# Probabilities kept in fp32, transposed by TensorE instead of by DMA, in an attention and expert kernel on one core

## The chip, the cores and the metric

One core of one Trainium2 chip. The metric is the device time of one execution in microseconds (us). Engines: TensorE (PE, its weight loads PEld), VectorE (DVE), ScalarE (ACT), GpSimd (POOL), SyncE (SP, whose queue issues all DMAs of this kernel).

## The reference

Attention over 4 batches, 8 heads, 1152 keys, head size 64, with the queries averaged in pairs (576 queries), and then a two-layer network with an ELU on the 2304 x 512 result (the weights arrive as 64-bit floats):

```python
q_pool = q.reshape(B, H, S // 2, 2, D).mean(axis=3)
scores = (1.0 / np.sqrt(D)) * np.matmul(q_pool, k.transpose(0, 1, 3, 2))
scores = scores - np.max(scores, axis=-1, keepdims=True)
attn = np.exp(scores)
attn = attn / (np.sum(attn, axis=-1, keepdims=True) + 1e-09)
x = np.matmul(attn, v)                      # then (B * 576, 512)
h = x @ w_in                                # 512 -> 2048
g = np.where(h > 0.0, h, np.exp(np.minimum(h, 0.0)) - 1.0)
out = g @ w_out                             # 2048 -> 512
```

## The kernel before

Each batch is a unit. A unit has 4 pairs of heads, a pair has 9 steps: 8 of 128 queries of one head (`st.h`, `st.t`) and one of the last 64 queries of both heads (`st.h is None`). That makes 144 steps. Operands of most matmuls are split in a high and a low fp16 half, and the products high x high, high x low, low x high are summed in PSUM.

`prep` (per pair) loads q, k and v, finds their scale (`absum` on ACT, `across`), splits them (`halves`: the high half on ACT, L429, the low one on DVE, L441, or POOL, L447) and transposes q and k by DMA (L519, L531).

`attention` (per step) runs, each as a task of its own:

1. `scores`: PE, L721, L726, L733, into the one PSUM tile `s`;
2. `biggest`: DVE, L739, scales `s` into SBUF (`ep`, fp32, 128x1152) and takes the row minimum;
3. `expo`: ACT, L745, the exponential in place with its row sum; `total`: ACT, L750; `recip`: DVE, L753;
4. `phi`: the normalised high half in fp16, on ACT (L764) or POOL (L756); `plo`: the low half, DVE, L759;
5. `ptr`: one DMA transpose of both halves (128 x 2304 fp16) into `pT`, issued on SP's queue (L783);
6. after every second step `pv`: PE, L822, L826, L832 (26 fp16 matmuls for 256 queries of a head), then `xa` (ACT, L844) and `xb` (DVE, L849), which add the two halves into `x32`.

`experts` works on a unit in two groups, 256 and 320 tokens: `m1` (L940, 12 matmuls for each 128 of the 2048 columns, fp16), the ELU (ACT L948 and L951, POOL L956, DVE L961, ACT L975 or POOL L983, POOL L979 or DVE L987), and `m2` (L1007, 48 matmuls for 128 tokens). It needs `x32` of all 8 heads, so the first unit's expert work starts when its attention is nearly done; from then on one unit's experts run beside the next unit's attention. `weights` and `split` decode the 64-bit weights (DVE L603, L604, L607; ACT L613, L649; DVE L652) in the opening.

The order on each engine's queue is fixed before the kernel runs: the class `Plan` places every task greedily by a key (its due time, from the constants in `CFG`), a booked duration and free buffers, and some tasks may go to one of two or three engines (`ways`). The tiles named `wo`, `g` and `h` in the trace are lent to each other: `ep` and `pT` of the first unit lie in buffers that later hold weights or activations (`wo`, `x16`).

PSUM: `s` takes three banks, and five banks `r` serve PV, `m1`, `m2` and `across`. SBUF: three `ep`, two `pT` buffers.

Of the kernel before, what the change touches and what calls it, by code (L numbers as in the profile page):

```python
# [18 lines left out]
    LOADS=130179, WI0=13938, WIT=6664, WO0=239437, WOT=10447, T0=3015, T1=1567, M0=7758,  # L19
    M1=49670, KS=33691, KM=2336, KE=12361, KH=7660, KL=-4056, KV=13470, KN=3968,  # L20
    KX=18983, KO=78603, PEN=600, W0L=-30160, WIN=1000, PD=18438, KS0=45563, KM0=5296,
    KE0=116348, KH0=-4488, KL0=-4155, KV0=2757, KX0=31516, PLM0=0, NS0=36, PLM=0,
    M2=24726, DP=0, FK=0, PENW=0, PENH=-3000, FL=2000, PH0=2, PH=1,
    PLP=1, WLP=1, HIP=0, PA=-715, PB=1180,
# [16 lines left out]
class Buf:  # L41


    def __init__(self, plan, tags):
        self.plan, self.tags, self.tag, self.users, self.slot, self.ap = plan, tags, tags[0], [], None, None


class Task:
    def __init__(self, eng, dur, key, emit, after, bufs):
        self.eng, self.dur, self.key, self.emit = eng, dur, key, emit  # L50
        self.ways = {eng: (dur, emit)}
        self.after = [a for a in after if a is not None]
        self.bufs = bufs
        self.pen = None
        self.kids, self.left, self.ready, self.end = [], 0, 0.0, None


class Plan:
# [4 lines left out]
    TAIL = {"PE": 70.0, "DVE": 75.0, "ACT": 90.0, "POOL": 30.0, "DMA": 0.0}  # L63

# [10 lines left out]
    def add(self, eng, dur, key, emit, after=(), bufs=(), ways=()):  # L75
        t = Task(eng, dur, key, emit, after, list(bufs))
        for e, d, f in ways:
            t.ways[e] = (d, f)
        for b in t.bufs:
            b.users.append(t)  # L80
        self.tasks.append(t)
        return t

    def _slots_for(self, t, now):
        taken = []
        for b in t.bufs:
            if b.slot is None:
                at = next(
                    (
                        (tag, j) for tag in b.tags for j, o in enumerate(self.slots[tag])  # L90
                        if (tag, j) not in [x for x, _ in taken]
                        and (o is None or all(u.end is not None and u.end <= now for u in o.users))
                    ),
                    None,
                )
                if at is None:
                    return None
                taken.append((at, b))
        return taken

    def run(self):
        order = []
        for n, t in enumerate(self.tasks):
            t.n = n
            t.left = len(t.after)
            for a in t.after:
                a.kids.append(t)
# [4 lines left out]
        landing, events = [], []  # L112
        for t in self.tasks:
            if t.left == 0:
                for e in t.ways:
                    wait[e].append(t)
        done = 0
        now = 0.0
        turn, used, cold, moved = self.WINDOW, 0.0, True, 0.0

# [6 lines left out]
        def finish(t, at):  # L127
            t.end = at
            for kid in t.kids:
                kid.left -= 1  # L130
                kid.ready = max(kid.ready, at + self.TAIL[t.eng] + (30.0 if t.eng == "DMA" else self.LAT[kid.eng]))
                if kid.left == 0:
                    for o in kid.ways:
                        wait[o].append(kid)
                    heapq.heappush(events, kid.ready)

        while done < len(self.tasks):
            again = True
            while again:
                again = False  # L140
                for e in engines:
# [3 lines left out]
                    for t in sorted((t for t in wait[e] if t.ready <= now), key=lambda t: (t.key, t.n)):  # L145
                        if e != t.eng:
                            ahead = rest[t.eng] if busy[t.eng] is not None else 0.0
                            ahead += sum(
                                o.dur for o in wait[t.eng]
                                if o.eng == t.eng and o.ready <= now + CFG["WIN"] and (o.key, o.n) < (t.key, t.n)  # L150
# [3 lines left out]
                        need = self._slots_for(t, now)  # L154
# [6 lines left out]
                    for (tag, j), b in need:  # L161
                        b.tag, b.slot = tag, j
                        self.slots[tag][j] = b
                    for o in t.ways:
                        wait[o].remove(t)
# [4 lines left out]
                    rest[e] = float(t.dur)  # L170
                    if e == "DMA":
# [13 lines left out]
            while events and events[0] <= now:  # L185
                heapq.heappop(events)
            if events:
                ends.append(events[0])
# [28 lines left out]
    def emit(self):  # L217
        for t in self.run():
            for b in t.bufs:
                if b.ap is None:  # L220
                    ap = self.make[b.tag](b.slot)
                    b.ap = ap if b.tag == b.tags[0] else self.lend[b.tags[0], b.tag](ap)
            t.emit()
# [3 lines left out]
def attention_moe_kernel(  # L227
# [22 lines left out]
    dr = ctx.enter_context(tc.tile_pool(name="dr", bufs=1, space=bass.MemoryType.DRAM))  # L250
# [8 lines left out]
    pool("v32", 1, [128, 2, NCH, D], F32)  # L259
# [25 lines left out]
    plan.lend["ep", "wo"] = lambda ap: whole(ap)[:, 0:3 * S]  # L285
    plan.lend["pT", "x16"] = lambda ap: whole(ap).rearrange("p (c s) -> p c s", s=256)
# [51 lines left out]
    for u in units:  # L338
# [9 lines left out]
        early = [(h, t) for h in range(2) for t in range(2)]  # L348
        late_ = [(h, t) for h in range(2) for t in range(2, u.nt)] + [(None, u.nt)]
# [37 lines left out]
    ones, tiny = wk[:, 60:61], wk[:, 61:62]  # L387
    make_identity(nc, ident)
    nc.vector.memset(ones, 1.0)
    nc.vector.memset(tiny, 1e-9 * 2.0 ** -15)  # L390
# [21 lines left out]
    kept = {}  # L412

    def prep(pr, t0, t1):
        u, p = pr.u, pr.p
        b, nq = u.b, u.nq
        q32, qn, qT, kT, v16, sm = (plan.buf(x) for x in ("q32", "qn", "qT", "kT", "v16", "sm"))
        pr.kT, pr.qT, pr.v16, pr.sm = kT, qT, v16, sm
# [59 lines left out]
        def plain(dst, src):  # L478
            return lambda: nc.sync.dma_start(out=dst(), in_=src())

# [7 lines left out]
        k_f, v_f = (lambda: kT.ap.rearrange("p h c s -> p (h c s)")), (lambda: v16.ap.rearrange("p h c e d -> p (h c e d)"))  # L488
# [4 lines left out]
        old = kept.get((b, p))  # L493
        nsum = 1 if old else 3
        if old is None:
            k32, v32, kn = (plan.buf(x) for x in ("k32", "v32", "kn"))
            k_s = lambda: k32.ap.rearrange("p h c d -> p (h c) d").rearrange("p (f t) d -> p f t d", t=2)
            k_h, k_l = (lambda: kn.ap[:, :, 0:4:3]), (lambda: kn.ap[:, :, 1:3])
            v_s, v_h, v_l = (lambda: v32.ap), (lambda: v16.ap[:, :, :, 0]), (lambda: v16.ap[:, :, :, 1])
            tk = plan.add("DMA", Move(500.0, 2400.0), lk, load(k, k32), (), [k32])  # L500
            tv = plan.add("DMA", Move(500.0, 2400.0), lk + 1, load(v, v32), (), [v32])
            sums.append(plan.add("ACT", act(1152) + 90.0, key[1], absum(k_h, k_s, 1), [tk], [kn, k32, sm]))
            sums.append(plan.add("ACT", act(1152) + 90.0, key[2], absum(k_h, v_s, 2), [tv, sums[1]], [kn, v32, sm]))

        def up(top):
# [3 lines left out]
            o = old[2].ap if old else a  # L509
            nc.vector.tensor_scalar(a[:, 0:nsum], a[:, 4:4 + nsum], 2.0 ** -14, None, op0=ALU.mult)  # L510
            ts(nc.vector, a[:, 12:13], a[:, 0:1], o[:, 1:2], -1.0 / (2.0 * float(D) ** 0.5))
            nc.vector.tensor_scalar(a[:, 13:14], o[:, 2:3], 2.0 ** -15, None, op0=ALU.mult)

        sms = [sm, old[2]] if old else [sm]
        sc = pr.sc = across(lambda: sm.ap[:, 0:nsum], nsum, key[3], sums + ([old[3]] if old else []), sms, up)
# [22 lines left out]
        if old:  # L538
            pr.kdone = [plan.add("DMA", Move(500.0, 2400.0), lk + 2, plain(k_f, lambda: old[0]), [old[4]], [kT])]
            pr.vdone = [plan.add("DMA", Move(500.0, 2400.0), lk + 3, plain(v_f, lambda: old[1]), [old[5]], [v16])]  # L540
            return
        kl = halves(1152, key[6], key[7], k_h, k_l, k_s, 1, [sc, sums[2]], [kn, k32, sm])
# [3 lines left out]
        if sum(o.b == b for o in units) > 1:  # L546
            kd = dr.tile([128, 2 * S], F16, name=f"kd{p}")
            vd = dr.tile([128, 2 * S], F16, name=f"vd{p}")
            kw = plan.add("DMA", Move(500.0, 2400.0), key[15], plain(lambda: kd, k_f), pr.kdone, [kT])
            vw = plan.add("DMA", Move(500.0, 2400.0), key[15], plain(lambda: vd, v_f), pr.vdone, [v16])  # L550
            kept[b, p] = (kd, vd, sm, pr.sc, kw, vw)
# [150 lines left out]
    def attention(st):  # L702
# [4 lines left out]
        def e_():  # L707
            return ep.ap[:, S:].bitcast(F32)

        def p_(j):  # L710
            return ep.ap[:, j * S:(j + 1) * S]
# [37 lines left out]
        def total():  # L749
# [321 lines left out]
```

## Time and profile before

| | |
|---|---|
| three runs | 938.51, 944.24 and 947.08 us, median 944.24 |
| span of the profiled execution | 938.4 us, from the first to the last instruction |
| busy share of the span | PE 78%, DVE 77%, ACT 74%, POOL 40% |
| DMA queue of SP | 156.01 MB, 80.8% of the 16 DMA engines |
| mean granted TensorE clock | 0.906 of full speed |

A share is a mean over three stages that differ: an opening of about 300 us (weights are decoded, attention of the first unit, little expert work), a middle of about 550 us (attention of one unit beside the experts of the one before), and an end of about 89 us (experts only). Busy PE time holds the time of the pipe's drain, so the distance between the starts of two stretches of matmuls tells the pace, not the sum of busy times.

### The profile page before, as it was taken

How to read it: one execution, taken by the hardware profiler on the slowest of the kernel's cores; microseconds unless marked ns; L12 is line 12 of the kernel's file. 1: busy time of each engine (PE TensorE's matmuls, PEld its weight loads, DVE VectorE, ACT ScalarE, POOL GpSimd, SP SyncE). 2: the span in 40 equal slices, each digit the busy share in tenths (PEclk: the TensorE clock that was granted, in tenths of full speed). 3: DMA queues.
4: the chain of work that ended last, by engine and by line, in shares of the span. 5: the costliest groups of instructions: out<-in, count | busy, mean ns of one | idle time of the engine just before them, and what ended most of it. 6: DMA issues, size and time to landing. Idle time of an engine off the chain costs nothing.

```text
span 938.4 us, 14749 instructions
## 1 busy us (share of the span) xinstructions
PE 733.5 (78%) x5283; PEld 428.6 (46%) x5283; DVE 724.7 (77%) x1235; ACT 690.8 (74%) x1169; POOL 375.4 (40%) x344
## 2 busy tenths in 40 slices
PE   0256455566939898998997989869978899689997
PEld 0123232333716455445644644438435544366563
DVE  5998999988998888878785886877777896785220
ACT  4587877877778889867777997568777987674460
POOL 3420513101637768402633881226324762043260
PEclk9998656756869999999998999979989999899999
DMA  7899999999957789897598989876799988754000
GB/s 236 223 200 202 236 227 246 236 190 264 199 138 163 125 169 200 164 198 140 105 201 179 199 175 206 170 152 105 156 214 201 168 159 177 136 102 76 23 1 28
DMA packets 434056, 156.94 MB, mean 167 GB/s; under 512 B 395840, under 2 KB 414272, under 8 KB 433984
## 3 DMA queue, kind: packets, MB, share of 16 engines
q1 hardware_dynamic: 433984, 156.01, 80.8%
q8 instruction: 41, 0.67, 0.3%
q14 instruction: 31, 0.25, 0.1%
HBM read 45.09 MB, written 4.72 MB: 53 GB/s over the span
## 4 chain that ended last, share of the span: by engine, by line
PE 25%; DVE 17%; DMA 15%; ACT 8%; issue 8%; POOL 5%; SPq 1%; DVEq 0%; POOLq 0%; ACTq 0%
DMA pT<-ep 12%; PE r L940 9%; PE r L1007 8%; DVE ep L739 7%; DVE ep L759 3%; ACT ep L745 3%; PE r L822 3%; PE s L721 2%; PE r L832 1%; POOL g L979 1%; PE s L733 1%; DMA kT<-kn 1%; ACT ep L764 1%; DVE tmp L961 1%; ACT tmp L951 1%
## 5 line engine op out<-in xcount | busy, mean ns | idle before, releaser
L745 ACT ACTIVATE ep<-ep,nm 128x1152 f32<-128x1152 f32 x132 | 165.2, 1251 | 75.1 <-DVE ep L739 55.7
L759 DVE SCALAR_TENSOR_TENSOR ep<-ep,nm 128x1152 f16<-128x1152 f32 x132 | 203.7, 1548 | 18.1 <-ACT ep L764 10.3
L739 DVE TENSOR_SCALAR_CACHE_REDUCE ep<-s,sm 128x1152 f32<-128x1152 f32 x132 | 186.4, 1412 | 38.1 <-DMA pT<-ep 24.4
L940 PE MATMUL r<-x,wi 128*128 128x256 f16 (+1 forms) x1536 | 201.6, 290 | 9.0 <-DVE x L849 5.1
L1007 PE MATMUL r<-wo,g 128*128 128x512 f16 (+1 forms) x864 | 176.1, 385 | 0.0
L721 PE MATMUL s<-kT,qT 128*128 128x512 f16 (+3 forms) x480 | 108.2, 366 | 86.1 <-DVE ep L739 67.9
L940 PEld LDWEIGHTS <-wi 128*128 128x128 f16 x1536 | 149.2, 99 | 56.9 <-issue 18.2
L764 ACT ACTIVATE ep<-ep,nm 128x1152 f16<-128x1152 f32 x111 | 138.3, 1247 | 22.3 <-DVE nm L753 22.0
L822 PE MATMUL r<-pT,v 128*128 128x256 f16 (+1 forms) x855 | 102.2, 272 | 35.3 <-DMA pT<-ep 19.8
L1007 PEld LDWEIGHTS <-g 128*128 128x128 f16 (+1 forms) x864 | 73.7, 102 | 87.9 <-issue 10.1
L956 POOL TENSOR_SCALAR tmp<-tmp,us 128x320 f32<-128x320 f32 (+1 forms) x96 | 73.3, 766 | 86.3 <-ACT tmp L951 86.1
L721 PEld LDWEIGHTS <-qT 128*128 128x128 f16 (+1 forms) x480 | 40.7, 105 | 138.9 <-issue 108.7
L822 PEld LDWEIGHTS <-v 128*128 128x128 f16 x864 | 70.3, 106 | 63.0 <-issue 29.3
L961 DVE SCALAR_TENSOR_TENSOR tmp<-r,wk,tmp 128x320 f32<-128x320 f32 (+1 forms) x96 | 57.5, 611 | 31.5 <-POOL tmp L956 31.1
L756 POOL TENSOR_SCALAR ep<-ep,nm 128x1152 f16<-128x1152 f32 x21 | 29.3, 1395 | 125.3 <-DVE nm L753 123.8
L979 POOL TENSOR_TENSOR g<-tmp,g 128x320 f16<-128x320 f32 (+1 forms) x70 | 70.9, 1019 | 12.6 <-ACT g L975 10.9
L384 POOL TENSOR_SCALAR q<-q,sm 128x576 f32<-128x576 f32 x14 | 12.6, 900 | 133.8 <-ACT qn L429 133.8
L948 ACT ACTIVATE tmp<-r 128x320 f32<-128x320 f32 (+1 forms) x96 | 46.5, 485 | 21.9 <-PE r L940 16.3
L733 PE MATMUL s<-kT,qT 64*128 64x512 f16 (+1 forms) x320 | 62.5, 432 | 0.0
L951 ACT ACTIVATE tmp<-tmp,us 128x320 f32<-128x320 f32 (+1 forms) x96 | 58.0, 609 | 1.3
L844 ACT ACTIVATE x<-r,sm 64x256 f32<-64x256 f32 (+1 forms) x96 | 39.9, 415 | 23.7 <-PE r L832 22.3
L832 PE MATMUL r<-pT,v 128*64 128x256 f16 (+1 forms) x760 | 56.9, 278 | 0.0
(128 smaller groups left out, 1041.8 us busy)
## 6 DMA issues: line engine op xcount, KB each, us to landing
k<-in_k_dram SPq DMA_DIRECT2D x16, 576.0 KB, 4.7
v<-in_v_dram SPq DMA_DIRECT2D x16, 576.0 KB, 4.6
q<-in_q_dram SPq DMA_DIRECT2D x32, 256.0 KB, 3.4
qT<-qT SPq DMA_DIRECT2D x48, 144.0 KB, 2.8
g<-in_moe_w_in_dram SPq DMA_DIRECT2D x13, 512.0 KB, 5.3
g<-in_moe_w_out_dram SPq DMA_DIRECT2D x13, 512.0 KB, 5.2
out_dram<-tmp SPq DMA_DIRECT2D x16, 256.0 KB, 2.7
pT<-ep SPq DMA_TRANSPOSE x130, 4.8
```

Source lines behind the costliest of these rows:

```text
L721: nc.tensor.matmul(s.ap[rows, c, 0:n], pr.qT.ap[:, 0, j, rows], keys[h][c], start=True, stop=False, skip_group_check=True,)
L733: nc.tensor.matmul(s.ap[rows, c, 0:512], pr.qT.ap[r, 1, j, rows], keys[h][c][r], start=False, stop=True, skip_group_check=True,)
L739: nc.vector.tensor_scalar(e_(), s.ap.rearrange("p a b -> p (a b)")[:, 0:S], pr.sm.ap[:, 12:13], None, op0=ALU.mult, op1=ALU.min, accum_out ...
L745: nc.scalar.activation(out=e_(), in_=e_(), func=AF.Exp, bias=nm.ap[:, 0:1], scale=-1.0, accum_out=nm.ap[:, 2:3],)
L759: nc.vector.scalar_tensor_tensor(out=p_(1), in0=e_(), scalar=nm.ap[:, 3:4], in1=p_(0), op0=ALU.mult, op1=ALU.subtract)
L764: nc.scalar.activation(out=p_(0), in_=e_(), func=AF.Copy, scale=nm.ap[:, 3:4])
L822: nc.tensor.matmul(x.ap[:, os], vt[:, order[c]].rearrange("p e d -> p (e d)"), pT.ap[:, c, cs], start=(c == 0), stop=False, skip_group_che ...
L940: nc.tensor.matmul(hp.ap[:, f * n:(f + 1) * n], w[:, a, c, (f0 + f) * 128:(f0 + f + 1) * 128], x16.ap[:, e, c, g0:g0 + n], start=(i == 0), ...
L951: nc.scalar.activation(out=en.ap[:, :m], in_=en.ap[:, :m], func=AF.Exp, scale=us.ap[:, 8 + g:9 + g])
L956: nc.gpsimd.tensor_scalar(en.ap[:, :m], en.ap[:, :m], -1.0, us.ap[:, 5:6], op0=ALU.add, op1=ALU.mult)
L979: nc.gpsimd.tensor_tensor(out=l, in0=gv, in1=h, op=ALU.subtract)
L1007: nc.tensor.matmul(op.ap[r0:r0 + tn, :], gt[qd].ap[:, a, fi, o:o + tn], w_out16(f // 2)[:, e, f % 2, :], start=(i < 128 // tn), stop=(i >= ...
```

## The change

- `expo` stays. `total` goes; `recip` adds the 1e-9 in an operation of its own. `phi` and `plo` go; one `norm` multiplies the fp32 probabilities in place, on POOL, or where POOL is behind on DVE or ACT.
- The DMA transposes `ptr` go. In their place each step has 9 TensorE transposes (fp32, 128 x 128, against the identity), three at a time into one PSUM bank `r`, and three copies (`out_act` or `out_dve`, 128 x 384 fp32) from there into `pT`.
- `pv` works in fp32 on the unsplit v: 18 matmuls for 128 queries of both heads, those of head 0 into PSUM partitions 0 to 63 and those of head 1 into 64 to 127. One copy per two steps (`xb` on DVE, or `xa`) replaces the pair `xa` and `xb`. The split of v goes from `prep` (one `absum`, one high and one low half per pair).
- Steps alternate between the two heads. `ep` has four fp32 buffers, `v32` three, `v16` goes.
- The plan: the constants are new; transposes that wait (`thin`) are woven one by one between the matmuls of an `m1` or `m2` task (`parts`) that is placed at that time, up to a quarter as many groups of three as that task has matmuls; a change of the array's tile mode is booked.

```diff
 CFG = dict(
-    LOADS=130179, WI0=13938, WIT=6664, WO0=239437, WOT=10447, T0=3015, T1=1567, M0=7758,
...
+    LOADS=-114467, WI0=33877, WIT=9245, WO0=755935, WOT=6543, T0=2082, T1=1393, M0=16194,
...
+        def weave(t, need):
...
+            for key, _, g in wait["PE"]:
+                if len(guests) >= len(host[0].parts) // 4:
+                    break
+                if g.thin and g is not t:
...
+            thin = [f for g in t.guests for f in g.thin]
+            for i, f in enumerate(t.parts):
+                if i < len(thin):
+                    thin[i]()
+                f()
...
-    pool("v16", 2, [128, 2, NCH, 2, D], F16)
-    pool("ep", 3, [128, 3 * S], F16)
+    pool("ep", 4, [128, S], F32)
-    pool("pT", 2, [128, 2 * NCH, 256], F16)
+    pool("pT", 2, [128, 2, NCH, 128], F32)
...
-        early = [(h, t) for h in range(2) for t in range(2)]
+        early = [(h, t) for t in range(2) for h in range(2)]
...
-        pr.vdone = [halves(1152, key[11], key[12], v_h, v_l, v_s, 2, [sc], [v16, v32, sm])]
+        pr.vdone = [tv]
...
         def recip():
+            nc.vector.tensor_scalar(nm.ap[:, 3:4], nm.ap[:, 2:3], 1e-9, None, op0=ALU.add)
             nc.vector.reciprocal(nm.ap[:, 3:4], nm.ap[:, 3:4])
...
         def norm_pool():
             nc.gpsimd.tensor_scalar(e_(), e_(), nm.ap[:, 3:4], 1.0, op0=ALU.mult, op1=ALU.mult)
+        def norm_dve():
+            nc.vector.tensor_scalar(e_(), e_(), nm.ap[:, 3:4], None, op0=ALU.mult)
...
-        def ptr():
-            nc.sync.dma_start_transpose(
-                out=pT.ap[:, :, half * 128:half * 128 + 128], in_=ep.ap[:, 0:2 * S]
-            )
...
+            def one(c, j=j, tp=tp):
+                nc.tensor.transpose(tp.ap[:, c * 128:(c + 1) * 128], e_()[:, (j + c) * 128:(j + c + 1) * 128], ident)
...
+            def out_act(j=j, tp=tp):
+                nc.scalar.activation(out=dst(j), in_=tp.ap[:, 0:384], func=AF.Copy)
+            def out_dve(j=j, tp=tp):
+                nc.vector.tensor_copy(dst(j), tp.ap[:, 0:384])
...
         def pv():
+            for c in range(NCH):
+                for h in range(2):
+                    order = [*range(h, 8, 2), *range(1 - h, 8, 2), 8]
+                    p = pT.ap[:, h, c] if st.h is not None else pT.ap[:, 0, c, 64 * h:64 * h + 64]
                     nc.tensor.matmul(
+                        x.ap[64 * h:64 * h + 64, 0:n], pr.v32.ap[:, h, order[c]], p,
+                        start=(c == 0), stop=(c == NCH - 1), skip_group_check=True,
                     )
...
         def xb():
+            nc.vector.tensor_copy(xdst(), x.ap[:, 0:n])
```

## Rows read from the trace of the kernel before

**Rows 1.** The head of the page: the span of the profiled execution.

```profile
span 938.4 us, 14749 instructions
```

**Rows 2.** Busy time by stage: stretch, length, PE, PEld, DVE, ACT, POOL (instructions), clock, DMA, GB/s.

```profile
0.00:300.00 300.00, 163.70 (x1056) 92.61 (x1057) 268.31 (x485) 224.18 (x380) 94.36 (x72) 0.78 0.93 212
300.00:850.00 550.00, 487.17 (x3685) 288.27 (x3684) 436.38 (x710) 433.42 (x724) 255.72 (x236) 0.96 0.85 164
850.00:939.00 89.00, 82.61 (x547) 47.69 (x544) 20.04 (x41) 33.22 (x67) 25.27 (x38) 0.98 0.15 34
```

**Rows 3.** The same stretches, `expo` alone (L745, ACT; two instructions per step).

```profile
0.00:300.00 300.00, 59.10 (x88) 0.78 0.93 212
300.00:850.00 550.00, 134.42 (x200) 0.96 0.85 164
```

**Rows 4.** The opening, `plo` alone (L759, DVE), then `phi` (L764, ACT).

```profile
0.00:300.00 300.00, 64.75 (x43) 0.78 0.93 212
0.00:300.00 300.00, 53.10 (x43) 0.78 0.93 212
```

**Rows 5.** The middle, `m1` (L940: PE, PEld), then `m2` (L1007).

```profile
300.00:850.00 550.00, 140.56 (x1079) 103.01 (x1080) 0.96 0.85 164
300.00:850.00 550.00, 148.72 (x716) 60.98 (x714) 0.96 0.85 164
```

**Rows 6.** Timeline of PE in the middle: start, length, line, shapes, count of matmuls.

```profile
328.86 0.65 PE L721 MATMUL s<-kT,qT 128*128 128x512 f16 x3
...
329.82 1.16 PE L822 MATMUL r<-pT,v 128*128 128x256 f16 x9
330.81 0.27 PE L826 MATMUL r<-pT,v 128*128 128x256 f16 x1
331.01 0.63 PE L832 MATMUL r<-pT,v 128*64 128x256 f16 x8
331.57 1.80 PE L940 MATMUL r<-x,wi 128*128 128x320 f16 x12
...
333.35 1.79 PE L940 MATMUL r<-x,wi 128*128 128x320 f16 x12
334.98 2.75 PE L1007 MATMUL r<-wo,g 128*128 128x512 f16 x12
```

**Rows 7.** Timeline of PE in the opening: one PV, then the next scores.

```profile
199.89 2.08 PE L822 MATMUL r<-pT,v 128*128 128x256 f16 x9 [2.68 <-DVE x L849]
...
203.11 1.14 PE L721 MATMUL s<-kT,qT 128*128 128x512 f16 x3
```

**Rows 8.** Groups by line and shape: busy us, mean ns, idle before.

```profile
L948 ACT ACTIVATE tmp<-r 128x320 f32<-128x320 f32 x64 | 27.6, 433 | 11.1 <-PE r L940 9.0 <-POOL g L979 1.0 <-POOL tmp L956 0.3
L948 ACT ACTIVATE tmp<-r 128x512 f32<-128x512 f32 x32 | 18.9, 590 | 10.9 <-PE r L940 7.3 <-DVE g L987 1.8 <-POOL g L979 1.5
L750 ACT ACTIVATE nm<-nm,wk 128x1 f32<-128x1 f32 x144 | 41.2, 286 | 1.6
L849 DVE SCALAR_TENSOR_TENSOR x<-r,sm,x 64x256 f32<-64x256 f32 x64 | 30.2, 472 | 11.7 <-ACT x L844 10.8
L429 ACT ACTIVATE v<-v,sm 128x1152 f16<-128x1152 f32 x16 | 19.9, 1242 | 1.3 <-PE r L832 1.3
L756 POOL TENSOR_SCALAR ep<-ep,nm 128x1152 f16<-128x1152 f32 x21 | 29.3, 1395 | 125.3 <-DVE nm L753 123.8 <-issue 1.4
```

**Rows 9.** Single lines of PE: duration in ns, least, median and greatest; the forms.

```profile
L397 PEld LDWEIGHTS r<-ident,sm x16: 81/81/86, 10.9 to 749.7; 128*3 128x3 f32 x16
L397 PE MATMUL r<-ident,wk x9: 270/371/373, 21.7 to 285.2; 128*1 128x128 f32 x9
L404 PEld LDWEIGHTS r<-xr,wk x66: 180/183/333, 13.3 to 877.3; 1*128 1x128 f32 x34, 3*128 3x128 f32 x32
L726 PE MATMUL s<-kT,qT x160: 218/219/314, 39.4 to 838.6; 128*128 128x128 f16 x128, 128*64 128x128 f16 x32
L822 PE MATMUL r<-pT,v x855: 189/272/421, 61.9 to 863.7; 128*128 128x256 f16 x113, 128*128 128x64 f16 x58
```

More of the change, by code (lines that the diff above doesn't have):

```diff
@@ L54, in __init__ @@
         self.pen = None
+        self.parts, self.thin, self.guests, self.modes = None, None, [], ("full", "full")
         self.kids, self.left, self.ready, self.end = [], 0, 0.0, None
@@ L79, in add, with _slots_for, _take @@
         for b in t.bufs:
-            b.users.append(t)
+            b.open += 1
+        t.modes = modes or t.modes
+        t.parts, t.thin = parts, thin
+        t.n = len(self.tasks)
         self.tasks.append(t)
         return t
-    def _slots_for(self, t, now):
-        taken = []
+    def _slots_for(self, t, used):
+        taken, mine = [], set()
         for b in t.bufs:
[L87 to L94, printed above, removed]
-                )
-                if at is None:
-                    return None
-                taken.append((at, b))
-        return taken
+            if b.slot is not None:
+                continue
+            at = None
+            for tag in b.tags:
+                for j, o in enumerate(self.slots[tag]):
+                    if (o is None or o.open == 0) and (tag, j) not in mine and (tag, j) not in used:
+                        at = (tag, j)
+                        break
+                if at is not None:
+                    break
+            if at is None:
+                return None
+            mine.add(at)
+            taken.append((at, b))
+        return taken
+    def _take(self, need):
+        for (tag, j), b in need:
+            b.tag, b.slot = tag, j
+            self.slots[tag][j] = b
     def run(self):
         order = []
[L103 to L107, printed above, removed]
         engines = ("PE", "DVE", "ACT", "POOL", "DMA")
@@ L111, in run @@
         rest = {e: 0.0 for e in engines}
-        landing, events = [], []
+        landing, coming = [], []
+        for t in self.tasks:
+            t.left = len(t.after)
+            for a in t.after:
+                a.kids.append(t)
         for t in self.tasks:
             if t.left == 0:
-                for e in t.ways:
-                    wait[e].append(t)
+                heapq.heappush(coming, (0.0, t.n, t))
         done = 0
@@ L119, in run @@
         turn, used, cold, moved = self.WINDOW, 0.0, True, 0.0
+        mode = "full"
         def shares():
@@ L128, in finish @@
             t.end = at
+            for b in t.bufs:
+                b.open -= 1
             for kid in t.kids:
@@ L144, in run @@
                     best = None
-                    for t in sorted((t for t in wait[e] if t.ready <= now), key=lambda t: (t.key, t.n)):
+                    for _, _, t in wait[e]:
                         if e != t.eng:
@@ L148, in run @@
                             ahead += sum(
-                                o.dur for o in wait[t.eng]
-                                if o.eng == t.eng and o.ready <= now + CFG["WIN"] and (o.key, o.n) < (t.key, t.n)
+                                o.dur for _, _, o in wait[t.eng]
+                                if o.eng == t.eng and (o.key, o.n) < (t.key, t.n)
+                            )
+                            ahead += sum(
+                                o.dur for r, _, o in coming
+                                if o.eng == t.eng and r <= now + CFG["WIN"] and (o.key, o.n) < (t.key, t.n)
                             )
@@ L153, in run @@
                                 continue
-                        need = self._slots_for(t, now)
+                        need = self._slots_for(t, ())
                         if need is not None:
@@ L160, in run @@
                     t, need = best
[L161 to L165, printed above, removed]
+                    guests = []
+                    if t.parts or t.thin:
+                        t, need, guests = weave(t, need)
+                    self._take(need)
+                    gone(t)
                     t.dur, t.emit = t.ways[e]
@@ L170, in run @@
                     rest[e] = float(t.dur)
+                    if e == "PE":
+                        if mode != t.modes[0]:
+                            rest[e] += self.SWITCH
+                        mode = t.modes[1]
+                    slow = 1.0 / self.COLD if cold else 1.0
+                    for i, (g, got) in enumerate(guests):
+                        self._take(got)
+                        gone(g)
+                        g.start = now
+                        t.guests.append(g)
+                        rest[e] += 3 * self.THIN
+                        heapq.heappush(landing, (now + slow * 3 * (i + 1) * (self.THIN + t.dur / len(t.parts)), g.n, g))
+                        done += 1
                     if e == "DMA":
@@ L184, in run @@
                 ends.append(landing[0][0])
[L185 to L188, printed above, removed]
+            if coming:
+                ends.append(coming[0][0])
             if not ends:
@@ L779, in attention @@
         pT = pr.pT
-        half = 0 if first else 1
-        def ptr():
-            nc.sync.dma_start_transpose(
-                out=pT.ap[:, :, half * 128:half * 128 + 128], in_=ep.ap[:, 0:2 * S]
-            )
-        ts_ = plan.add("PE", 950.0 if st.h is not None else 1100.0, t0 - K("KS", u), scores, pr.kdone + [pr.qs], [s, pr.kT, pr.qT])
-        tm = plan.add("DVE", 1345.0, t0 - K("KM", u), biggest, [ts_, pr.sc], [s, nm, ep, pr.sm])
-        te = plan.add("ACT", 1255.0, t0 - K("KE", u), expo, [tm], [nm, ep])
@@ L790, in attention @@
-        to = plan.add("ACT", 200.0, t0 - K("KE", u), total, [te], [nm])
-        tr = plan.add("DVE", 90.0, t0 - K("KE", u), recip, [to], [nm])
-        hp, ha = ("POOL", pol(S), phi), ("ACT", act(S), phi_act)
-        ld = ("DVE", dve(S), plo)
-        every = K("PLM", u)
-        slow = every and st.i % every == every - 1 and (u.i > 0 or st.i < CFG["NS0"])
-        if slow or K("PH", u) == 2:
-            hp, ha = ha, None
-        elif K("PH", u) == 1:
-            hp, ha = ha, hp
-        th = plan.add(hp[0], hp[1], t0 - K("KH", u), hp[2], [tr], [ep, nm], [ha] if ha else [])
```

259 lines of the change are left out of this document (121 added, 138 removed).

## The prediction

> **What bounds the kernel now.** I read three views: busy time by stage, then single lines in the same stages, then the timeline of PE for its pace. By stage [rows 2], the opening (0 to 300 us) has DVE busy 268 of 300 us, ACT 224, PE 164, and the DMA engines at 0.93; the middle (300 to 850 us) has PE busy 487 of 550 us at a clock of 0.96, with DVE and ACT near 435 and DMA at 0.85; the end (89 us) is PE alone, 83 us. So the opening hangs on DVE (and on the DMA transposes), the middle on PE with three other resources close behind it, the end on PE. The reader is to see that one share for the whole span hides this: an edit that unloads DVE, ACT and DMA and loads PE can shorten the opening, and must be paid for in the middle.
>
> `expo` issues two instructions per step, so the opening holds 88 / 2 = 44 steps and the middle 100 [rows 3].
>
> **The pace of PE at full clock**, from start to start [rows 6]: scores of a step 329.82 - 328.86 = 0.96 us; PV of two steps 331.57 - 329.82 = 1.75; 12 matmuls of 320 columns 334.98 - 333.35 = 1.63, that is 0.136 each and, by columns, 0.109 for 256 (PV's nine take (330.81 - 329.82) / 9 = 0.110) and 0.218 for 512. In the middle that makes: scores 100 x 0.96 = 96; PV 50 x 1.75 = 88; `m1` 1079 x 0.123 (half of them 256 wide) = 132; `m2` 716 [rows 5], of which the code gives a fifth (the last 64 tokens) two at a time: 716 x (0.8 x 0.218 + 0.2 x 0.109) = 141; about 10 for small ones: 467 of 550 us, a fill of 0.85. The rest is waiting, drains and slow clock.
>
> **The change, part by part.**
>
> *Opening, DVE and ACT.* DVE loses `plo`, 65 us [rows 4], and `xb`, some 20 x 0.47 = 9 [rows 8]; it gains one one-column operation per step (44 x 0.15, half of what L750's takes on ACT, as an estimate = 7) and the small x copies (22 x 0.25 = 5): 268 - 74 + 12 = 206. ACT loses `phi` 53 [rows 4], `total` 44 x 0.286 = 13, `xa` about 9 (as `xb`), and for five pairs the two passes over v at about 1.25 each (L429's 1242 ns) = 13 [rows 8]: 224 - 88 = 136. New are 44 x 3 = 132 copies of 128 x 384 from PSUM. ACT's reads of PSUM take 433 ns for 320 columns and 590 for 512 [rows 8], so 433 + 64 x 157 / 192 = 485 ns for 384: 64 us, on either engine. Sum 206 + 136 + 64 = 406, or 203 each if shared evenly. DVE is busy 0.89 of the opening now; at that share the opening takes 203 / 0.89 = 228 us. It can't be under 203.
>
> *POOL* gets `norm`: 1.4 us a step as L756 [rows 8], 44 x 1.4 = 62 on top of 94, 156 of 228 us; in the middle 140 on top of 256 less its few `phi`. POOL hides it; without that cover DVE would take it over. A step's chain gets longer (norm, transposes, copies), but four `ep` buffers let four steps be under way, and a step comes only every 5 us.
>
> *DMA.* 144 transposes of 590 KB go, 85 of the 156 MB. What SP's queue had behind them (loads of q, k, v, weights, the transposes of q and k) comes earlier. I book no gain of its own: DVE's sum already sets the opening. The late load of v costs nothing as long as its three buffers are ahead of PV.
>
> *Transposes on PE.* 9 a step, 900 in the middle. The trace shows single fp32 ones only, in `across`: 270 ns at full clock and 371 at the low one, 101 apart, where 128 fp16 columns are 96 apart (218, 314) and 256 columns 149 (272, 421) [rows 9]. So it streams its 128 columns once, and its pace is half of a 256-column matmul's 0.110: 0.055 us, the bound from below. Its load is the fp32 one of 128 columns: 180 ns against 81 for three columns, so some 0.10 us of streaming [rows 9]. Between two `m1` or `m2` matmuls of 0.11 to 0.22 us the load is covered, and 0.055 stands; back to back the load sets 0.10; if loads don't overlap at all, 0.18. I take 0.06 in the middle, where nearly each transpose finds an `m1` or `m2` task, and 0.10 in the opening, where there is hardly any: 900 x 0.06 = 54 us, bounds 50 and 162.
>
> A rule speaks against this. The Trainium skill (TensorE: Matmul & The Clock Gate, Part 4: PE-mode transpose) says that a transpose takes about 275 ns in a kernel and that it doesn't count as activity for the clock. The trace agrees with the first as a latency (270), and no run here shows the second. Two of the rivals below are what these would mean here.
>
> *PV in fp32.* 18 calls for two steps. One fp32 call is two loads and two matmuls (66 for the 33 calls of L404) [rows 9], so 36 matmuls of 128 columns. L832 shows two column halves side by side: 8 matmuls of 256 columns within 0.63 us, or (0.63 - 0.27) / 7 = 0.051 from one to the next, with a 64-column load each [rows 6]. One pass per matmul, side by side: 36 x 0.055 / 2 = 0.99; but the 36 loads at 0.051 need 1.84 already; two passes, side by side: 36 x 0.11 / 2 = 1.98; two passes, one after the other: 3.96. I take 1.98, nearest to the loads: 50 x 1.98 = 99 instead of 88.
>
> *Middle.* 96 + 99 + 132 + 141 + 10 + 54 = 532 us of PE. DVE and ACT together fall from 870 to about 280 + 250 + 300 x 0.485 = 676 (DVE less 156 of `plo`, 27 of `xb`; ACT less 100 of `phi`, 57 of `total` and `xa`, 28 of v), 60% of each, and DMA is out of the way. So PE alone bounds, and its fill rises, I take to 0.94, what the end shows (about 84 of 89): 532 / 0.94 = 566.
>
> *End.* The same work, 89 us.
>
> **Sum:** 228 + 566 + 89 = 883 against the span of 938.4 [rows 1]. The span stands 5.8 us under the runs' median of 944.24, so 889 as a median. The whole gain comes from the opening; the middle pays for itself.
>
> **The rivals.**
>
> 1. *The opening stays at the low clock.* PV with its scores takes 203.11 - 199.89 = 3.22 us at the low clock [rows 7] against 1.75 at full: 1.84 times. A step would need (0.96 + 0.99 + 9 x 0.10) x 1.84 = 5.25 us of PE; 44 of them 231, with 228 `m1` matmuls 0.123 x 1.84 = 52 more: 283. Then PE, not DVE, sets the opening: 283 + 566 + 89 + 6 = 944. For it: the clock there is 0.78 over PE busy 164 of 300 [rows 2]. Against it: PE that has no gaps got the full clock in the middle. Chance 0.08.
> 2. *The middle fills no better than now*, because transposes, copies and PV wait for one another in PE's fixed order, and what stands behind them waits too: 532 / 0.85 = 626; 228 + 626 + 89 + 6 = 949. For it: more and shorter tasks, five `r` banks for one more user. Chance 0.10.
> 3. *fp32 PV doesn't run side by side.* That is slower: 99 us more of PE, (532 + 99) / 0.94 = 671; 228 + 671 + 89 + 6 = 994. It decides from about 0.6 us per PV on. For it: no fp32 pair is in the trace. Against it: the fp16 pairs of L832. Chance 0.10.
> 4. *Each transpose costs its latency*, 0.27: (478 + 243) / 0.94 = 767, in all 1090. Against it: L726 takes 218 ns alone, and matmuls follow at a fraction of such latencies. Chance 0.04.
>
> **How the numbers follow.** The forecast case has 0.66, and by itself reaches from 203 + 543 + 89 + 6 = 841 (even split, fill 0.98) to 250 + 590 + 89 + 6 = 935 (transposes at 0.10 for half). 0.02 is left for what I don't see. Within 1% of 944 (about what can be told from no change) end rivals 1 and 2 mostly. Faster by over 1% 0.68, within 1% 0.17, slower 0.15. The range takes in rivals 1 and 2: 838 to 952.
>
> **What would show it.** Right: expert work starts 60 to 70 us earlier than now; DMA share under a half; PE above 0.9 busy at a clock near 1 from there on; woven transposes 0.05 to 0.06 us apart from their neighbours; a PV within about 2 us; DVE and ACT near 60%. Wrong: PV of 4 us (rival 3); PE waiting for copies (ACT or DVE) or for `norm` on POOL in the middle (rival 2); an opening with PE busy all the time at a clock near half (rival 1). The sum fails above all if the opening does not shrink, for there the gain lies.

## The result and the profile after

The changed kernel takes 928.62 us as a median (926.55 to 930.06), the kernel before in the same session 944.70 (938.51 to 947.08): a ratio of 0.9845 with an interval of 0.9809 to 0.9881. It is 1.6% faster, where 889 us, 5.9% faster, had been forecast. The head of the page of the changed kernel, its row of busy times, its DMA queue, and its chain of work by engine:

```profile
span 926.4 us, 19421 instructions
PE 855.7 (92%) x7731; PEld 611.8 (66%) x7731; DVE 598.2 (65%) x1325; ACT 589.2 (64%) x1114; POOL 390.6 (42%) x387
q1 hardware_dynamic: 97600, 71.06, 30.7%
PE 76%; DVE 12%; DMA 5%; ACT 3%; issue 2%; POOL 1%; SPq 1%; ACTq 0%; DVEq 0%; POOLq 0%
```

Busy time by stage, columns as in [rows 2], cut where about the same amount of work is done as before at 300 and at 850 us (between the cuts lie 102 steps, 1103 `m1` and 672 `m2` matmuls; before 100, 1079 and 716):

```profile
0.00:242.00 242.00, 179.55 (x1692) 130.46 (x1693) 212.84 (x463) 174.99 (x348) 129.89 (x109) 0.99 0.56 151
242.00:846.00 604.00, 600.73 (x5520) 436.85 (x5518) 361.04 (x812) 382.99 (x706) 248.57 (x258) 1.00 0.25 57
846.00:927.00 81.00, 75.46 (x524) 44.45 (x522) 24.28 (x51) 31.23 (x61) 12.09 (x21) 0.99 0.05 17
```

So the opening went from 300 us to 242, the end from 89 to 81, and the middle from 550 to 604: 58 + 8 - 54 = 12 us of span. The middle is PE and nothing else: 601 of 604 us busy, clock 1.00, DMA at 0.25, DVE and ACT near 60%. What PE waits for, in the opening (0 to 200 us) and then in the middle (242 to 846), as line, releaser, us in total, times, longest; the longest entries of each:

```profile
PE r L462 <- DVE wk L666: 24.1, 4, 10.3
PE s L761 <- DVE ep L779: 15.8, 16, 4.1
...
PE r L820 <- ACT pT L832: 1.6, 4, 1.0
PE s L761 <- DVE ep L779: 1.0, 2, 0.8
```

In the middle PE hardly waits for anyone. So what the middle takes is what PE's instructions cost, and the timeline of PE prices them: transposes (L820) woven between `m1` (L949) and between `m2` (L1021) matmuls, a PV of two steps (L851) up to the next scores (L761), nine transposes in a row (and, as a row of its own, the last seven of them), and a PV of the last 64 queries:

```profile
92.31 0.39 PE L773 MATMUL s<-kT,qT 64*128 64x512 f16 x2
92.64 1.20 PE L820 MATMUL r<-ident,ep 128*128 128x128 f32 x9
...
92.91 0.93 PE L820 MATMUL r<-ident,ep 128*128 128x128 f32 x7
...
93.77 1.27 PE L851 MATMUL r<-pT,v 128*64 128x64 f32 x36
...
502.45 0.27 PE L820 MATMUL r<-ident,ep 128*128 128x128 f32 x1
502.56 0.30 PE L949 MATMUL r<-x,wi 128*128 128x320 f16 x1
502.70 0.27 PE L820 MATMUL r<-ident,ep 128*128 128x128 f32 x1
...
504.34 2.19 PE L851 MATMUL r<-pT,v 128*64 128x128 f32 x36
506.46 0.66 PE L761 MATMUL s<-kT,qT 128*128 128x512 f16 x3
...
523.40 0.27 PE L820 MATMUL r<-ident,ep 128*128 128x128 f32 x1
523.51 0.38 PE L1021 MATMUL r<-wo,g 128*128 128x512 f16 x1
523.72 0.27 PE L820 MATMUL r<-ident,ep 128*128 128x128 f32 x1
...
646.38 1.27 PE L851 MATMUL r<-pT,v 128*64 128x64 f32 x36
647.58 0.33 PE L820 MATMUL r<-ident,ep 128*128 128x128 f32 x1
```

From transpose to transpose lie 502.70 - 502.45 = 0.25 us with a 320-column matmul between (0.136 by itself [rows 6]) and 523.72 - 523.40 = 0.32 with one of 512 columns (0.218): a woven transpose costs 0.11 us, not 0.06. Averaged over five in a run it is 0.108. Nine in a row take 93.77 - 92.64 = 1.13, or 0.126 each, but the surplus lies at the two ends: the first two take 92.91 - 92.64 = 0.27 behind scores that use 64 rows of the array (L773), the last 0.20 ahead of a PV that uses 64 columns, and those between follow each other after (0.93 - 0.27) / 6 = 0.11 us, as the woven ones do. The PV takes 506.46 - 504.34 = 2.12.

The groups of the new lines, as in [rows 8]:

```profile
L794 POOL TENSOR_SCALAR ep<-ep,nm 128x1152 f32<-128x1152 f32 x139 | 178.7, 1286 | 286.7 <-DVE nm L791 181.1
L820 PE MATMUL r<-ident,ep 128*128 128x128 f32 x1296 | 273.9, 282 | 6.0 <-ACT x L860 1.7
L832 ACT ACTIVATE pT<-r 128x384 f32<-128x384 f32 x334 | 153.8, 489 | 121.2 <-PE r L820 119.3
L835 DVE COPY pT<-r 128x384 f32<-128x384 f32 x98 | 53.7, 553 | 19.9 <-PE r L820 19.0
```

The copies cost what was forecast (489 ns on ACT against 485; 553 on DVE), `norm` on POOL less (1286 ns against 1.4 us). A transpose's record lasts 282 ns, but that is its latency (and the profile models where a matmul's record ends): it does not tell the pace.

### The profile page after: what moved, and what is told of

It reads as the page before. It is cut to its first block, busy times and chain, and to the rows that moved or that the text cites. A ratio compares the mean times of both kernels' runs of the same rounds, so it can differ in the third digit from the quotient of the medians.

```text
span 926.4 us, 19421 instructions
## 1 busy us (share of the span) xinstructions
PE 855.7 (92%) x7731; PEld 611.8 (66%) x7731; DVE 598.2 (65%) x1325; ACT 589.2 (64%) x1114; POOL 390.6 (42%) x387
## 3 DMA queue, kind: packets, MB, share of 16 engines
q1 hardware_dynamic: 97600, 71.06, 30.7%
## 4 chain that ended last, share of the span: by engine, by line
PE 76%; DVE 12%; DMA 5%; ACT 3%; issue 2%; POOL 1%; SPq 1%; ACTq 0%; DVEq 0%; POOLq 0%
PE r L949 18%; PE r L1021 17%; PE r L820 14%; PE r L851 14%; PE s L761 7%; PE s L773 4%; DVE ep L779 3%; DMA kT<-kn 3%; DMA qT<-qn 2%; DVE tmp L646 1%; DVE g L649 1%; DVE tmp L645 1%; ACT ep L785 1%; PE s L766 1%; PE r L469 1%
## 5 line engine op out<-in xcount | busy, mean ns | idle before, releaser
L794 POOL TENSOR_SCALAR ep<-ep,nm 128x1152 f32<-128x1152 f32 x139 | 178.7, 1286 | 286.7 <-DVE nm L791 181.1
L820 PE MATMUL r<-ident,ep 128*128 128x128 f32 x1296 | 273.9, 282 | 6.0 <-ACT x L860 1.7
L949 PE MATMUL r<-x,wi 128*128 128x256 f16 (+1 forms) x1536 | 242.0, 286 | 1.7 <-ACT x L860 1.6
L832 ACT ACTIVATE pT<-r 128x384 f32<-128x384 f32 x334 | 153.8, 489 | 121.2 <-PE r L820 119.3
L820 PEld LDWEIGHTS r<-ident,ep 128*128 128x128 f32 x1296 | 166.5, 142 | 48.8 <-issue 30.0
L1021 PE MATMUL r<-wo,g 128*128 128x512 f16 (+1 forms) x792 | 180.5, 380 | 0.0
L949 PEld LDWEIGHTS <-wi 128*128 128x128 f16 x1536 | 153.0, 100 | 24.7 <-issue 0.8
L851 PE MATMUL r<-pT,v 128*64 128x128 f32 (+1 forms) x2880 | 160.0, 265 | 1.5 <-ACT pT L832 1.5
L851 PEld LDWEIGHTS r<-pT,v 128*64 128x64 f32 x2880 | 142.6, 137 | 20.4 <-issue 12.1
L761 PE MATMUL s<-kT,qT 128*128 128x512 f16 (+2 forms) x480 | 97.2, 334 | 17.6 <-DVE ep L779 16.8
L1021 PEld LDWEIGHTS <-g 128*128 128x128 f16 (+1 forms) x792 | 69.5, 102 | 62.7 <-issue 1.8
L761 PEld LDWEIGHTS <-qT 128*128 128x128 f16 (+1 forms) x480 | 39.6, 101 | 54.7 <-issue 27.7
L835 DVE COPY pT<-r 128x384 f32<-128x384 f32 x98 | 53.7, 553 | 19.9 <-PE r L820 19.0
L773 PE MATMUL s<-kT,qT 64*128 64x512 f16 (+1 forms) x320 | 57.8, 398 | 0.0
L1002 DVE TENSOR_TENSOR g<-tmp,g 128x320 f16<-128x320 f32 (+1 forms) x56 | 33.5, 604 | 19.7 <-ACT g L990 14.9
```

Source lines behind the costliest of these rows:

```text
L761: nc.tensor.matmul(s.ap[rows, c, 0:n], pr.qT.ap[:, 0, j, rows], keys[h][c], start=True, stop=False, skip_group_check=True,)
L773: nc.tensor.matmul(s.ap[rows, c, 0:512], pr.qT.ap[r, 1, j, rows], keys[h][c][r], start=False, stop=True, skip_group_check=True,)
L794: nc.gpsimd.tensor_scalar(e_(), e_(), nm.ap[:, 3:4], 1.0, op0=ALU.mult, op1=ALU.mult)
L820: nc.tensor.transpose(tp.ap[:, c * 128:(c + 1) * 128], e_()[:, (j + c) * 128:(j + c + 1) * 128], ident)
L832: nc.scalar.activation(out=dst(j), in_=tp.ap[:, 0:384], func=AF.Copy)
L851: nc.tensor.matmul(x.ap[64 * h:64 * h + 64, 0:n], pr.v32.ap[:, h, order[c]], p, start=(c == 0), stop=(c == NCH - 1), skip_group_check=True,)
```

## The experiments

The theory after the first look: the middle is PE alone, and the forecast sold it 900 transposes at half their price. Rivals: the price comes from the weaving or from loading the fp32 weights, not from the streaming; the plan, which books 58 ns for a woven transpose, is misled by the true price; the opening, set by DVE, or its late start holds the time, so that cheaper transposes would bring little.

**Every third transpose left out** (same order of work).

```diff
-            thin = [lambda c=c, one=one: one(c) for c in range(3)]
+            thin = [lambda c=c, one=one: one(c) for c in range(2)]
```

> Every third transpose is left out (432 of 1296), the copies move 256 instead of 384 columns, and PV reads the chunk before in place of the missing one, so the probabilities of a third of the keys are wrong. The order of all tasks is that of the changed kernel. Theory 'from 200 us on PE is full and a microsecond of PE is a microsecond': about 327 of the 432 lie there, 327 x 0.108 = 35 us, so 928 becomes about 893 (881 if those of the opening count as well). Rival 'waits between engines': less than 10 us.

Measured 893.84 us (891.05 to 897.28), ratio to before 0.9497 (0.9455 to 0.9540). The middle of this kernel:

```profile
300.00:800.00 500.00, 496.50 (x4558) 345.84 (x4555) 303.50 (x717) 310.98 (x615) 211.21 (x217) 1.00 0.25 60
```

928.62 - 893.84 = 35 us for a third of the roughly 981 transposes that come after 200 us: 35 / 327 = 0.107 us each, the timeline's price. PE stays full (496.5 of 500 us), so the middle is paid by PE's own work, transpose by transpose. The starts of the expert work bear this out: the first `m1` matmul comes at 180.5 us instead of 182.0, the last at 861.7 instead of 895.1, so nearly all of the gain lies behind the opening. The narrower copies can't have made it, since the changed kernel's PE waits for copies for 1.6 us only in the middle.

**Transposes of fp16 probabilities**: `norm` writes fp16, the copies widen to fp32 again; `ep` has three buffers instead of four, `v32` two.

```diff
-            nc.gpsimd.tensor_scalar(e_(), e_(), nm.ap[:, 3:4], 1.0, op0=ALU.mult, op1=ALU.mult)
+            nc.gpsimd.tensor_scalar(h_(), e_(), nm.ap[:, 3:4], 1.0, op0=ALU.mult, op1=ALU.mult)
...
-                nc.tensor.transpose(tp.ap[:, c * 128:(c + 1) * 128], e_()[:, (j + c) * 128:(j + c + 1) * 128], ident)
+                nc.tensor.transpose(t16(tp)[:, c * 128:(c + 1) * 128], h_()[:, (j + c) * 128:(j + c + 1) * 128], ident16)
```

> The norm writes the probabilities as fp16 and the transposes run in fp16 (the copies widen them to fp32 again, PV stays fp32), so the probabilities are rounded to fp16; three ep and two v32 buffers, since the room for the fp16 copy is taken from there. Theory 'PE is full and the fp32 transpose is its new load': a transpose falls from 0.108 to about 0.055 us, 1296 x 0.053 = 69 us less work of PE, and the time falls from 928 to 860 to 875. Rival 'waits for copies and norm set the time, PE only looks full': less than 25 us are gained.

Measured 902.19 us (901.68 to 905.32), ratio to before 0.9575 (0.9535 to 0.9614). The timeline of PE, then the stretches 0 to 200 and 300 to 800 us:

```profile
508.94 0.22 PE L828 MATMUL r<-ident,ep 128*128 128x128 f16 x1
509.00 0.38 PE L1029 MATMUL r<-wo,g 128*128 128x512 f16 x1
509.22 0.22 PE L828 MATMUL r<-ident,ep 128*128 128x128 f16 x1
...
518.09 0.68 PE L828 MATMUL r<-ident,ep 128*128 128x128 f16 x9
...
0.00:200.00 200.00, 122.68 (x1206) 82.37 (x1206) 171.84 (x391) 137.46 (x281) 88.95 (x80) 0.90 0.59 168
300.00:800.00 500.00, 487.22 (x4902) 325.96 (x4898) 316.65 (x730) 328.10 (x611) 228.68 (x235) 1.00 0.25 61
```

An fp16 transpose costs 509.22 - 508.94 - 0.218 = 0.06 us woven and (0.68 - 0.22) / 8 = 0.06 in a row: the forecast's price, but for operands of 2 bytes instead of 4. The gain, 26 us, is less than 1296 x 0.05 = 65. Three parts of the gap can be read: the transposes ahead of 200 us, about a quarter, lie where PE has time to spare (16 us of the 65); the first 200 us got less done (24 `m1` matmuls against 88, 35 steps against 37), some 11 us of PE; and PE is busy 487 of 500 us where the changed kernel has 497. The first expert matmul starts at 197.4 us instead of 182.0, so the opening lost 15 us. Whether the slower opening comes from the third `ep` buffer or from its clock (0.90 against 0.99) isn't told apart.

**Only 64 queries of each transpose** (the fp32 load keeps its 128 columns, the moving side has 64; each result is copied twice, so half of the probabilities is replaced by the other half).

```diff
-                nc.tensor.transpose(tp.ap[:, c * 128:(c + 1) * 128], e_()[:, (j + c) * 128:(j + c + 1) * 128], ident)
+                nc.tensor.transpose(tp.ap[:, c * 128:c * 128 + 64], e_()[0:64, (j + c) * 128:(j + c + 1) * 128], ident[0:64, 0:64])
```

> Only the first 64 of a step's 128 queries are transposed (64 moving columns of the identity, while the load stays 128 columns of fp32); the copies read those 64 twice, so the result is not the attention of all queries. Read is the pace of transposes that stand in a row of nine. Theory 'stream' (an fp32 transpose moves its columns at half pace): 0.109 falls to about 0.055 us each. Theory 'load' (the fp32 load of 128 columns, some 0.10 us, is never covered): it stays at 0.10 to 0.11. The time of the whole kernel: stream, down by up to 1296 x 0.054 = 70 us less what the change of the array's rows costs among woven ones; load, no change.

Measured 1075.22 us, one run: slower, which neither theory had. Nine in a row, then three woven ones:

```profile
92.44 0.71 PE L820 MATMUL r<-ident,ep 64*128 64x64 f32 x9
...
502.73 0.27 PE L820 MATMUL r<-ident,ep 64*128 64x64 f32 x1
502.94 0.39 PE L1028 MATMUL r<-wo,g 128*128 128x512 f16 x1
503.26 0.27 PE L820 MATMUL r<-ident,ep 64*128 64x64 f32 x1
```

In a row they settle the question: a record lasts 0.22 us here, so they follow each other after (0.71 - 0.22) / 8 = 0.06 us, against 0.11 with 128 columns. The load has 64 rows instead of 128, but its 128 columns and its length are the same (a median of 136 ns against 141). So it is not the load that sets the price but the moving columns, at 0.11 us per 128 of fp32 against 0.06 of fp16 ((0.68 - 0.22) / 8). Woven, a pair takes 503.26 - 502.73 = 0.53 us where the full transposes need 0.32. What differs is that these use 64 rows of the array and the matmuls around them all 128: the change there and back costs about 0.53 - 0.218 - 0.06 = 0.25 us. The Trainium skill (TensorEngine Tiling (Array Packing), Tiling Modes, Key Properties) says that a change of the tiling mode drains the engine. This run fits that and gives a price; the drain itself stands in no view.

**No weaving**: transposes only as groups of their own.

```diff
-                    if t.parts or t.thin:
+                    if False:
```

> The transposes are never put between the matmuls of m1 and m2: each group of three is a task of its own, and the plan is made anew. Theory 'a transpose costs PE 0.108 us wherever it stands': the same time within 1% (919 to 938). Rival 'weaving covers half of each transpose', as the plan books it (3 x 58 against 335 ns): slower by about 900 x 0.05 = 45 us or more, 970.

Measured 949.09 us (947.17 to 952.86), ratio to before 1.0080 (1.0050 to 1.0111), 2.2% above the changed kernel; neither expectation had that. PE's timeline in it, then the first nine of the 18, and the ninth with the tenth, as rows of their own:

```profile
505.00 2.44 PE L820 MATMUL r<-ident,ep 128*128 128x128 f32 x18
507.27 0.57 PE L949 MATMUL r<-x,wi 128*128 128x320 f16 x3
...
505.00 1.20 PE L820 MATMUL r<-ident,ep 128*128 128x128 f32 x9
...
505.93 0.59 PE L820 MATMUL r<-ident,ep 128*128 128x128 f32 x2
```

On average a transpose of this row costs 2.27 / 18 = 0.126, a woven one 0.108, but the pace is the same: the first takes 0.165 us, behind the scores, the others of the first nine follow after 0.109, and between the ninth and the tenth, which is the next step's, PE pauses (0.29 us from start to start). Over all transposes that start behind 200 us, the median distance to PE's next matmul is 109 ns in both kernels, and the mean is 134 ns here against 120 woven; for some 980 of them that makes 13 of the 20 us. So weaving hides nothing of a transpose's streaming, where the prediction's 0.06 against 0.10 and the plan's booking of 58 ns against 112 have it hide about half. What it saves are the ends of such rows and the pauses between them. What causes the pauses, and where the other 7 us went, isn't shown.

**A woven transpose booked at 108 ns.**

```diff
-    SWITCH, THIN = 94.0, 58.0
+    SWITCH, THIN = 94.0, 108.0
```

> One number of the plan: a woven transpose is booked at 108 ns instead of 58, so the order is made with the true price. Theory 'PE is full in any order': within 1% of 928. Rival 'the order is wrong because the booking is': faster by 1 to 3%, 900 to 918.

Measured 932.42 us (930.54 to 934.68), ratio to before 0.9894 (0.9845 to 0.9943): within half a per cent of the changed kernel. With the true price the plan found no cheaper order (its other constants stayed as they were), so the wrong booking isn't where the gain went.

**A DVE instruction of about 0.65 us added to each step**, ahead of `recip`, in the same order.

```diff
         def recip():
+            nc.vector.tensor_reduce(dve_x, ep.ap[:, 0:576], axis=AX.X, op=ALU.max)
```

> A reduction over 576 columns more on DVE in each step, some 0.65 us, in the same order; its result is not used. Theory 'PE is the bound, DVE only in the opening': the 37 steps of the first 200 us pay, the other 107 don't: 928 plus 5 to 25, 933 to 953. Rival 'the chain of a step (biggest, exp, norm) sets the time': 144 x 0.65 = 94 more, 1020.

Measured 952.92 us (950.78 to 953.45), ratio to before 1.0122 (1.0093 to 1.0151): 24 us above the changed kernel. The group of the added instruction, 50 to 100 us of the opening, and the `m1` matmuls of the changed kernel and of this one (the range of times is that of their first and last start):

```profile
L791 DVE TENSOR_REDUCE wk<-ep 128x1 f32<-128x576 f32 x144 | 107.8, 749 | 44.1 <-ACT ep L786 43.1
...
50.00:100.00 50.00, 37.45 (x361) 26.77 (x360) 47.89 (x104) 35.75 (x70) 24.19 (x19) 1.00 0.53 128
...
L949 PE MATMUL r<-x,wi x1536: 269/290/310, 182.0 to 895.1; 128*128 128x256 f16 x96, 128*128 128x320 f16 x96
...
L951 PE MATMUL r<-x,wi x1536: 269/290/310, 195.2 to 917.7; 128*128 128x256 f16 x96, 128*128 128x320 f16 x96
```

DVE's busy time rose from 598.2 to 681.8 us, that is 84 or 0.58 a step (a record lasts 0.75, but its end overlaps with the next); of these 84 us 24 cost time. In the changed kernel 37 steps lie ahead of 200 us: 37 x 0.58 = 21, or 28 with 0.75. That is near the 24, but the starts put them elsewhere: the first expert matmul comes 195.2 - 182.0 = 13.2 us later, the last 917.7 - 895.1 = 22.6. So the opening pays for more than half of its added work and not for all of it, and the 107 steps behind it, with some 62 us of added work, pay about 9. DVE counts most in the opening, and little, but not nothing, where PE is full.

**The loads of q, k and v early**, as the constant of the kernel before has them.

```diff
-    LOADS=-114467, WI0=33877, WIT=9245, WO0=755935, WOT=6543, T0=2082, T1=1393, M0=16194,
+    LOADS=130179, WI0=33877, WIT=9245, WO0=755935, WOT=6543, T0=2082, T1=1393, M0=16194,
```

> One constant of the plan: the loads of q, k and v come before those of w_in, as in the kernel before, and the plan is made anew. The first scores of the changed kernel start at 44.6 us, those of the kernel before at 38.4. Theory 'PE's late start costs its full length': 5 to 10 us faster, 918 to 924. Rival 'the opening is set by DVE and ACT, an earlier start only moves the wait': 925 to 932.

Measured 937.73 us (936.42 to 939.80), ratio to before 0.9945 (0.9924 to 0.9967): slower than the changed kernel by 1%, though the first scores start at 37.18 us instead of 44.64. Both expectations missed. The first expert matmul comes at 195.3 us instead of 182.0. From 200 to 242 us in this kernel, then in the changed one:

```profile
200.00:242.00 42.00, 36.62 (x354) 27.97 (x353) 40.46 (x76) 33.64 (x66) 25.05 (x23) 0.96 0.54 129
...
200.00:242.00 42.00, 40.25 (x355) 28.85 (x354) 38.25 (x76) 32.10 (x57) 33.42 (x29) 1.00 0.21 52
```

With the early loads DVE is busy 40.5 of 42 us there and PE only 36.6; in the changed kernel it is 38.3 and 40.3. An earlier start doesn't shorten the sum of DVE's work: what gave way was probably still to be done at the other end. One constant moves many tasks, so this run doesn't show the cause.

**Probabilities and v as single fp16 in PV**, on top of the fp16 transposes: one pass instead of two, no halves, coarser than the split operands of the kernel before.

```diff
-                        x.ap[64 * h:64 * h + 64, 0:n], pr.v32.ap[:, h, order[c]], p,
+                        x.ap[64 * h:64 * h + 64, 0:n], pr.v16.ap[:, h, order[c]], p,
```

> As the run with fp16 transposes, and the copies keep the probabilities in fp16, v is rounded to fp16 (one pass per pair, on POOL or ACT), and PV runs on single fp16 operands: probabilities and v are rounded to fp16. PV of two steps falls from 2.12 to about 0.55 us of PE. Theory 'PE is the bound and stays it': some 53 of the 72 lie behind 200 us, 53 x 1.57 = 83 us, so 902 becomes about 820. Rival 'DVE, ACT and POOL are next': it stops at 850 to 875, with PE no longer full.

Measured 842.67 us (840.53 to 844.49), ratio to before 0.8954 (0.8925 to 0.8983), 59.5 us less than with fp16 transposes alone. A PV, what follows it, and the middle:

```profile
407.36 0.69 PE L873 MATMUL r<-pT,v 128*64 128x128 f16 x18
407.98 0.23 PE L840 MATMUL r<-ident,ep 128*128 128x128 f16 x1
...
300.00:800.00 500.00, 469.15 (x4290) 292.86 (x4289) 310.85 (x730) 357.68 (x674) 238.27 (x244) 0.99 0.25 61
```

The PV went from 2.12 to 407.98 - 407.36 = 0.62 us. Of the some 53 x 1.50 = 80 us that this takes from PE after 200 us, 59.5 came out as time; PE is busy 469 of 500 us now and begins to wait for the other engines. The time lies between the two expectations, 820 and 850. This version is faster than both kernels; its price is the rounding of probabilities and v to one fp16.

## Why the prediction was off

**Right: what bounds it, and that the gain comes from the opening.** Most points of the prediction's list show: DMA share 30.7% (under a half), PE full at a clock of 1.00 from 200 us on, DVE and ACT at 65% and 64%, a PV of 2.1 us. Two don't: expert work starts at 182.0 us where the trace of before has 234.5, so 52 us earlier where 60 to 70 were said, and woven transposes stand 0.11 us from their neighbours and not 0.05 to 0.06. None of the four rivals happened: the opening's clock is 0.99 (rival 1), PE waits for 3 us in the middle (rival 2), PV is side by side (rival 3), a transpose doesn't cost its latency (rival 4).

**Wrong: the price of a transpose.** The middle by the measured paces, with the counts of 242 to 846 us: scores 102 x 0.96 = 98; PV 46 x 2.12 + 12 x 1.20 = 112; transposes 934 x 0.108 = 101; `m1` 1103 x 0.123 = 136; `m2` 672 x 0.196 = 132; small ones 10: 589 us, against 532 forecast. 47 of these 57 are the transposes (101 against 54), 13 PV (112 against 99), the rest evens out. The fill was better than taken, 589 / 604 = 0.975 against 0.94, which gave 23 us back: 532 / 0.94 = 566 became 604. With 0.108 in the forecast's own sum the middle would have been (532 + 900 x 0.048) / 0.94 = 612 instead of 566, and the whole 935, 1% faster than before in place of 5.9%. That this lies near the 928.62 measured is in part luck: of the other misses, the opening (14 us) and PV (13 / 0.94 = 14) cost about what the fill (23) and the end (8) gave back.

The step that failed is the one from latencies to a pace. Single fp32 transposes of before were 101 ns longer at the low clock than at full, 128 fp16 columns 96 [rows 9], and from that one pass at 0.055 was read. The runs show 0.109, woven and in a row. The difference of a latency between two clocks therefore doesn't tell how long the array is held. Two things at hand would have told it. The trace of before had the pace itself, from start to start, in a single transpose of `across` between two matmuls of `m2`:

```profile
383.91 0.27 PE L397 MATMUL r<-ident,sm 128*3 128x128 f32 x1
384.02 1.24 PE L1007 MATMUL r<-wo,g 128*128 128x512 f16 x5
```

PE's next matmul starts 384.02 - 383.91 = 0.11 us after it; six such transposes between `m1` or `m2` matmuls show 0.108 to 0.110, a seventh 0.135. Their load has one or three columns (81 ns for three [rows 9]), so the load of 128 columns has no part in this price. And the prediction had the number already: for PV it took two records per fp32 call at 0.11 us each, and came out near (2.12). A transpose is one record of the same kind, fp32 with 128 columns, and should have had the same 0.11. The bound from above, 162 us, was right to be kept; the value was taken from the wrong end.

**PV.** 1.98 forecast, 2.12 measured, the right choice for a wrong reason, which is luck: it was taken as the nearest to what the loads need. But the PV of 64 queries, with as many loads, takes 647.58 - 646.38 = 1.20 us, so the 36 loads at 0.051 (1.84 us) are no floor; the streaming sets it. (The 3.22 us of the prediction's first rival are the PV alone, up to the next scores, as the 1.75 beside them are.)

**The opening.** 228 forecast, 242 measured. It was reckoned from DVE and ACT shared evenly, 203 each. Measured at 242 us are 213 and 175, in sum 388 (406 forecast), but not even: of the first 118 copies 97 went to ACT, and DVE is still the longer one. DVE's 213 / 0.88 = 242, with the share of 0.89 that was taken; the even split failed, not the sum. The run with more work on DVE shows that its work counts there, though not in full: 13 us at the first expert matmul, for some 20 added.

**The end.** 81 against 89: 8 us better than taken; no run was spent on it.

**Together**: 14 (opening) + 38 (middle) - 8 (end) = 44 of span, 883 against 927, which is the miss of the time but for 4 us in what lies around the span.

**The rule weighed in the prediction.** The granted clock of the changed kernel is 1.00 from 200 us on, with nine transposes in each step, and 0.99 over the opening, where they are a fifth of PE's matmuls (357 of 1692). Over the first 200 us it was lower, 0.90 and 0.81, in the two kernels whose transposes or PV took less of PE's time (PE busy 123 and 112 of the 200 us, against 139). The Trainium skill (TensorE: Matmul & The Clock Gate, Part 4: PE-mode transpose) has transposes not count as activity for the clock. No run here shows a loss from them, but none tries them alone: the longest row of the changed kernel has 24. Its 275 ns is right as a latency (282 here).

**What stays open.** The new constants of the plan were not undone as a whole: one of them alone is worth 1% (the early loads), and how much of the opening's 58 us is theirs and how much is the work taken off DVE, ACT and DMA isn't separated.

## What to carry to other kernels

Take a pace from start to start of neighbours of the same type and width; a record's length, or how it changes with the clock, is a latency. One such neighbour in the trace of before was enough to see the price. Work moved from three engines to PE is paid in full as soon as PE is the only bound, so price each new PE instruction by its columns and its type before counting what the others gain, and look at the type first: fp32 here costs twice of fp16 per column in a transpose. And where one engine fills a stage and another the next, ask of each saving in which stage it lies: 84 us of added DVE work cost 24, and a third of the transposes was worth only what lay behind 200 us.

## What the runs showed of the hardware beyond that

- fp32 moves at half the pace of fp16 in a transpose: 0.109 us against 0.06 for 128 columns, in a row as woven, although both are one record, with nearly the same length (0.27 and 0.22).
- Two fp32 matmuls on the two column halves of the array run side by side: 36 records of 128 columns in 2.12 us; and in fp16 18 in 0.62.
- Woven between matmuls of all 128 rows, a transpose that uses 64 rows costs 0.31 us where one of 128 rows costs 0.108: half the work for three times the price. In a row the same transpose costs 0.06, so the rest goes with the change of rows there and back.
